# Sparse attention with a mixture of experts: preparation copies on GpSimd, and the first batch's causal mask as a matmul

## The chip, the cores and the metric

The kernel runs on one core of one Trainium2 chip. The metric is the device time of one execution in microseconds (us), and the median of several runs is compared. The engines are named as in the profile: PE is TensorE (PEld its weight loads), DVE is VectorE, ACT is ScalarE, POOL is GpSimd, and SP issues most DMAs. Each engine works through its own queue in order; semaphores tie the queues together.

## The reference

There are 4 batches of 8 heads with 768 positions of 64 features. Keys stand in 24 chunks of 32. A query takes only the 6 chunks with the highest upper bound of a score, and of these only keys that are not later than itself:

```python
ub = np.sum(np.maximum(q[:, :, :, None, :] * k_min[:, :, None, :, :], q[:, :, :, None, :] * k_max[:, :, None, :, :]), axis=-1)
top_chunks = np.argsort(np.where(causal, ub, -1e9), axis=-1)[..., -top_k:]
mask = sel & (pos[:, None] >= pos[None, :])
attn = softmax(np.where(mask, scale * q @ k.T, -1e9))
x = (attn @ v).transpose(0, 2, 1, 3).reshape(B * S, H * D)
y_dense = np.maximum(x @ w1_dense, 0.0) @ w2_dense
y_moe[e's tokens] = gate_w * (np.maximum(x @ w1[e], 0.0) @ w2[e])    # e: the best of 8 experts by x @ w_gate
return y_dense + y_moe
```

## The kernel before, in words

**Pairs and units.** Two heads are worked on together as a pair, so there are 16 pairs (`NP`), four per batch (`HP`). The scores of a pair are cut into 11 units of up to 512 columns. Units 0, 5 and 6 hold the diagonal blocks of 128 x 128, where the causal mask cuts through; each of them has four such blocks. For a unit PE computes the scores (line 551), ACT the exponential (555), POOL zeroes later keys in a diagonal unit with a select (557), and PE multiplies with the values (570). The main loop runs over all units; it starts the scores two units ahead and finishes a unit, with the value product, one unit late.

**Chunk selection without a mask of its own.** The score matmul has 128 rows of contraction: 64 features and, in the other 64 rows, 24 rows of chunk membership. `kT[i][g]` holds the keys of head g in one half and the membership table `exf` in the other; `rT[i][g]` holds the negated queries in one half and, in the other, a flag for each chunk that was not selected. Thus a key of an unselected chunk gets a large positive score, and the exponential with scale -0.125 makes it zero. There are three buffers of each (`NB`), used by pair p modulo 3. The membership rows are written once at the start (`expand`, 144 and 145).

**Preparation.** Pair p+2 is prepared while pair p runs. POOL casts k, q and v to f16 (469, 471, 476). `prep_k` transposes the keys on PE (482), ACT copies them from PSUM into `kp` (484), and DVE reduces every chunk to its maximum and minimum, `ks` (495), and multiplies them with a mask of halves into `kb` (498). `prep_q` transposes the queries (510); ACT writes their positive part `qp` (513), and DVE writes the negated queries into `rT` (514 for all 128 partitions, 515 for the second head's half). `prep_kt` copies both halves of `kp` into `kT` on DVE (502, 503). `prep_ub` computes the bounds on PE (525), finds the sixth largest with DVE (531) and writes the flags (533). `prep_s`, a pair later, transposes the flags (539) and copies them into `rT` (541, 542).

**Other work in the loop.** A finished pair is normalized on DVE (579, 581). The dense layer and the gate of a batch are mixed as small pieces into the units of the next batch. POOL also scatters the tokens into a table by expert (370), issues the expert weights' loads (206), and builds the routing constants once (171 to 186). After the attention the experts' blocks run; their results are scattered by POOL (733).

**Order.** A scheduler of the language orders each engine's instructions from the program order, with its own estimates of duration. `tc.issue_after(latest["pool"].ins)` ties the casts and the table scatters behind the POOL instruction that the program made last, which before is the select of line 557.

## Time and profile before

| | |
|---|---|
| time, median of 3 runs | 255.95 us (254.11 to 255.99) |
| the profiled execution's own time | 257.31 us |
| its span, first to last instruction | 255.5 us |
| mean granted clock of TensorE | 0.993 |
| busy: PE / DVE / ACT / POOL | 213.7 / 179.3 / 176.1 / 159.6 us |
| DMA | 50.12 MB moved |

Busy time is what an engine's instructions took; PE's is modelled, because matmuls are pipelined. A group of instructions is one source line with its operation and shapes; behind it stand the busy time, the mean duration of one in ns, the idle time of the engine just ahead of them, and what ended that idle time. The chain of waits is followed back from the last instruction to whatever released each step. In a timeline row the first two numbers are the start and the duration in us.

### The profile page before, as it was taken

Reading aid. Unit: us, or ns where it says so; the run is one execution under the profiler, and the core shown is the slowest. Engines: PE = TensorE matmul, PEld = TensorE weight load, DVE = VectorE, ACT = ScalarE, POOL = GpSimd, SP = SyncE. Lnnn points to the kernel's source line nnn. Section 1 sums busy time; section 2 is a strip of 40 time slices with the busy share of each in tenths; the row PEclk is TensorE's granted clock in tenths of the full one; section 3 lists DMA queues with packets and bytes.
Section 4 is the critical chain, followed back from the end, with each engine's and each line's share of the span. In section 5 each row is a group of like instructions: output and inputs, shape, how many; then the busy total and the mean of one; then the engine's idle time right before and its main releaser. Section 6 shows DMA issues by size and latency. Waiting matters only on the chain.

```text
span 255.5 us, 7236 instructions
## 1 busy us (share of the span) xinstructions
PE 213.7 (84%) x2547; PEld 141.8 (55%) x2547; DVE 179.3 (70%) x558; ACT 176.1 (69%) x332; POOL 159.6 (62%) x198
## 2 busy tenths in 40 slices
PE   0378969888989899999988988889769999999970
PEld 0256746656657576766567755555335554555530
DVE  6869989999979689998898895167223345555540
ACT  2799979878779898878889778815356555455440
POOL 4746998566276987168986145514744463887881
PEclk9999999999999999999999999999999999999997
DMA  6999999999999799989999924447879999787885
GB/s 172 262 267 228 217 227 239 220 232 202 239 174 292 132 276 226 250 179 242 298 230 258 190 72 128 144 114 218 234 154 208 220 209 200 124 140 97 117 112 105
DMA packets 75124, 50.12 MB, mean 196 GB/s; under 512 B 29648, under 2 KB 68176, under 8 KB 75088
## 3 DMA queue, kind: packets, MB, share of 16 engines
q1 hardware_dynamic: 59856, 30.33, 46.9%
q0 software_dynamic: 15232, 19.32, 45.6%
q8 instruction: 21, 0.34, 0.6%
q14 instruction: 15, 0.12, 0.1%
HBM read 41.93 MB, written 18.23 MB: 235 GB/s over the span
## 4 chain that ended last, share of the span: by engine, by line
PE 29%; DVE 22%; POOL 18%; issue 10%; DMA 7%; ACT 6%; SPq 3%; another core or an unknown queue 1%; POOLq 0%; DVEq 0%; ACTq 0%
DVE ks L495 7%; POOL out_dram L733 7%; PE hp L696 6%; PE yp L725 6%; PE hp L385 4%; POOL ex L557 3%; PE yp L394 3%; POOL table L370 2%; SPq L92 2%; DMA vf<-in_v_dram 2%; ACT ex L555 2%; ACT kp L484 2%; DVE kT L503 2%; DMA kf<-in_k_dram 2%; PE sp L551 2%
## 5 line engine op out<-in xcount | busy, mean ns | idle before, releaser
L555 ACT ACTIVATE ex<-sp 128x512 f16<-128x512 f32 (+1 forms) x176 | 90.9, 608 | 8.9 <-PE sp L551 4.6
L551 PE MATMUL sp<-rT,kT 128*128 128x128 f16 (+3 forms) x384 | 64.4, 260 | 4.0 <-ACT ex L555 2.7
L733 POOL DMA_INDIRECT out_dram<-yo,xg x28 | 43.3, 1545 | 23.5 <-DVE yo L732 9.8
L557 POOL TENSOR_SCALAR_AFFINE_SELECT ex<-ex 128x512 f16<-128x512 f16 x48 | 32.6, 694 | 36.9 <-ACT ex L555 30.8
L570 PE MATMUL op<-v,ex 128*128 128x65 f16 x672 | 48.4, 194 | 3.3 <-POOL ex L557 1.8
L570 PEld LDWEIGHTS <-ex 128*128 128x128 f16 x672 | 36.9, 98 | 19.0 <-POOL ex L557 6.4
L370 POOL DMA_INDIRECT table<-xbig,slot x24 | 23.9, 997 | 20.2 <-issue 15.1
L732 DVE TENSOR_SCALAR yo<-yp,xg 128x512 f32<-128x512 f32 x27 | 20.3, 751 | 22.2 <-PE yp L725 13.3
L551 PEld LDWEIGHTS <-kT 128*128 128x128 f16 x384 | 29.0, 98 | 7.7 <-issue 4.2
L725 PE MATMUL yp<-we,ehT 128*128 x112 | 28.7, 379 | 3.9 <-ACT ys L397 2.5
L707 ACT COPY ehT<-tp 128x512 f16<-128x512 f16 x28 | 16.4, 585 | 21.5 <-PE tp L705 16.7
L696 PE MATMUL hp<-we,exT 128*128 x112 | 29.1, 379 | 2.0 <-DMA xg<-table 1.2
L495 DVE TENSOR_REDUCE ks<-kp 128x24 f16<-128x768 f16 x30 | 27.3, 943 | 4.2 <-ACT kp L484 3.9
L385 PE MATMUL hp<-xT,wd 128*128 128x384 f16 x128 | 26.2, 325 | 0.8 <-DVE xT L258 0.8
L699 ACT ACTIVATE eh<-hp 128x512 f16<-128x512 f32 x28 | 16.7, 597 | 11.4 <-PE hp L696 10.1
L394 PE MATMUL yp<-wd,hT 128*128 128x512 f16 x96 | 23.9, 379 | 0.3 <-issue 0.3
L690 DVE COPY exT<-tp 128x512 f16<-128x512 f16 x28 | 11.8, 423 | 17.4 <-PE tp L688 9.9
L387 ACT ACTIVATE hT<-hp 128x384 f16<-128x384 f32 x32 | 16.1, 505 | 9.0 <-PE hp L385 6.2
L397 ACT COPY ys<-yp 128x512 f32<-128x512 f32 x24 | 14.3, 598 | 9.5 <-PE yp L394 4.3
L484 ACT COPY kp<-pk 128x768 f16<-128x768 f16 x16 | 12.9, 806 | 8.8 <-PE pk L482 8.8
L581 DVE TENSOR_TENSOR xbig<-op,rs 128x384 f16<-128x384 f32 x32 | 17.5, 547 | 0.2
L725 PEld LDWEIGHTS <-ehT 128*128 128x128 f16 x112 | 10.1, 98 | 12.6 <-issue 2.8
(127 smaller groups left out, 383.1 us busy)
## 6 DMA issues: line engine op xcount, KB each, us to landing
we<-in_moe_w_dram POOLq DMA_DIRECT2D x16, 512.0 KB
kf<-in_k_dram SPq DMA_DIRECT2D x32, 192.0 KB
qf<-in_q_dram SPq DMA_DIRECT2D x32, 192.0 KB
vf<-in_v_dram SPq DMA_DIRECT2D x32, 192.0 KB
out_dram<-ys SPq DMA_DIRECT2D x48, 128.0 KB
xg<-table SPq DMA_DIRECT2D x28, 136.0 KB
table<-zt SPq DMA_DIRECT2D x9, 136.0 KB
wd<-in_moe_w_dense_dram POOLq DMA_DIRECT2D x2, 512.0 KB
```

The costliest lines, as they stand in the source:

```text
L370: sc = nc.gpsimd.indirect_dma_start(out=table, out_offset=bass.IndirectOffsetOnAxis(ap=keep["slot"][:, t : t + 1], axis=0), in_=xbig[b % 2 ...
L385: nc.tensor.matmul(hp, wd[:, ko, j * 128 : (j + 1) * 128], xT[:, ko, g * G * 128 : (g + 1) * G * 128], start=(ko == 0), stop=(ko == NK - 1))
L394: nc.tensor.matmul(yp, hold["h"][:, j, i * 128 : (i + 1) * 128], wd[:, NK + j], start=(j == 0), stop=(j == NK - 1))
L495: nc.vector.tensor_reduce(out=ks[:, i], in_=kp.rearrange("d (c w) -> d c w", w=32), op=op, axis=mybir.AxisListType.X)
L551: nc.tensor.matmul(sp[:, o : o + w], kT[p % NB][g][:, kt * 128 : (kt + 1) * 128], rT[p % NB][g][:, a * 128 : z * 128], start=(o == 0), sto ...
L555: nc.scalar.activation(ex[:, 0:o], sp[:, 0:o], AF.Exp, scale=-0.125)
L557: latest["pool"] = nc.gpsimd.affine_select(out=ex, in_=ex, compare_op=ALU.is_ge, fill=0.0, base=0, pattern=[[0, 4], [1, 2], [2, 64]], chan ...
L570: nc.tensor.matmul(s["op", g][:, t * (D + 1) : (t + 1) * (D + 1)], ex[:, o : o + 128], v16[p % NB][:, g, kt, :], start=first, stop=(last_o ...
L696: nc.tensor.matmul(hp, s["xT"][:, ko], wef[:, bass.ds(offs[i] + ko * 512, 512)], start=(ko == 0), stop=(ko == NK - 1))
L725: nc.tensor.matmul(yp, s["hT"][:, j], wef[:, bass.ds(offs[i] + (NK + j) * 512, 512)], start=(j == 0), stop=(j == NK - 1))
L732: nc.vector.tensor_scalar(o, yp, gate, None, ALU.mult)
L733: sc = nc.gpsimd.indirect_dma_start(out=out, out_offset=to, in_=o, in_offset=None, bounds_check=N - 1, oob_is_err=False, compute_op=ALU.by ...
```

## The change

It has four parts.

1. In the first batch (pairs 0 to 3) the causal mask of a diagonal unit is added to the scores by one more matmul, of the identity with a table `later` that holds 30000 where the key is later than the query. It is repeated four times by its access pattern, so it covers 512 columns. The select on POOL goes for these pairs. From pair 4 on the select stays.
2. The keys are no longer written to a tile of their own, `kp`, but into `kT[..][1]`, all 128 partitions. From there the first head's half is copied to `kT[..][0]`: by POOL for pairs 1 to 3, by DVE for pair 0 and from pair 4 on. The first head's keys in `kT[..][1]` are then partly covered by the 32 membership rows; that copy from `exf` is made anew for each pair, by ACT for pair 0 and by POOL for the others. The rows that are left over meet zeros in `rT`.
3. The negated queries are written once, for all 128 partitions, into `rT[..][1]`. For pair 0 DVE writes the first head's half from PSUM again, and ACT computes the positive part as before. From pair 1 on DVE computes the positive part `qp` from `rT[..][1]` in SBUF, and POOL copies the first head's half to `rT[..][0]`. The third term of the bounds reads `rT[..][1]`.
4. With that go three memsets and three copies of `expand`. `latest["pool"]` now can also be one of the new POOL copies.

```diff
+    later = acst.tile([128, 128], HF)
+    nc.vector.memset(later, 0.0)
+    nc.gpsimd.affine_select(out=later, in_=later, compare_op=ALU.is_ge, fill=30000.0, base=0,
+                            pattern=[[1, NJ], [NJ, 64]], channel_multiplier=-1)
...
-            s["kp"] = kp = ahead.tile([128, S], HF, name="kp")
+            kp = kT[p % NB][1]
...
         def prep_kt(p):
-            kp = st[p]["kp"]
-            nc.vector.tensor_copy(kT[p % NB][0][0:64], kp[0:64])
-            nc.vector.tensor_copy(kT[p % NB][1][64:128], kp[64:128])
+            k0, k1 = kT[p % NB]
+            if p:
+                (nc.gpsimd if p < HP else nc.vector).tensor_copy(k0[0:64], k1[0:64])
+                latest["pool"] = nc.gpsimd.tensor_copy(k1[0:32], exf[0:32])
+            else:
+                nc.vector.tensor_copy(k0[0:64], k1[0:64])
+                nc.scalar.copy(k1[0:32], exf[0:32])
...
-            nc.scalar.activation(qp, pq, AF.Relu)
-            nc.vector.tensor_single_scalar(r0, pq, -1.0, ALU.mult)
-            nc.vector.tensor_single_scalar(r1[64:128], pq[64:128], -1.0, ALU.mult)
+            if p:
+                nc.vector.tensor_single_scalar(r1, pq, -1.0, ALU.mult)
+                nc.vector.tensor_scalar(qp, r1, -1.0, 0.0, ALU.mult, ALU.max)
+                latest["pool"] = nc.gpsimd.tensor_copy(r0[0:64], r1[0:64])
+            else:
+                nc.scalar.activation(qp, pq, AF.Relu)
+                nc.vector.tensor_single_scalar(r1, pq, -1.0, ALU.mult)
+                nc.vector.tensor_single_scalar(r0[0:64], pq[0:64], -1.0, ALU.mult)
...
+            diag = pc[0][1] == pc[0][2]
+            added = diag and p < HP
+            if added:
+                nc.tensor.matmul(sp.rearrange("p (n k) -> p n k", k=128), ident, later.unsqueeze(1).to_broadcast([128, 4, 128]),
+                                 start=True, stop=False, skip_group_check=True)
...
-            if pc[0][1] == pc[0][2]:
+            if diag and not added:
                 latest["pool"] = nc.gpsimd.affine_select(out=ex, in_=ex, compare_op=ALU.is_ge, fill=0.0, base=0,
```

More of the change, by code (lines that the diff above doesn't have):

```diff
@@ L133 @@
         nc.vector.memset(kT[i][0][64:128], 0.0)
-        nc.vector.memset(kT[i][1][0:64], 0.0)
         nc.vector.memset(v16[i][:, :, :, D : D + 1], 1.0)
@@ L551, in scores @@
                 nc.tensor.matmul(sp[:, o : o + w], kT[p % NB][g][:, kt * 128 : (kt + 1) * 128],
-                                 rT[p % NB][g][:, a * 128 : z * 128], start=(o == 0), stop=True, skip_group_check=True)
+                                 rT[p % NB][g][:, a * 128 : z * 128], start=(o == 0 and not added), stop=True,
+                                 skip_group_check=True)
                 o += w
```

5 lines of the change are left out of this document (2 added, 3 removed).

## The prediction

> **What bounds the kernel now.** I read the totals first, then the busy time by stretch, the waits, and the chain of waits.
>
> ```profile
> PE 213.7 (84%) x2547; PEld 141.8 (55%) x2547; DVE 179.3 (70%) x558; ACT 176.1 (69%) x332; POOL 159.6 (62%) x198
> ```
>
> The totals mix stages with different limits. The busy time by stretch separates them; columns are PE, PEld, DVE, ACT and POOL.
>
> ```profile
> core 0: us, PE busy (x) PEld busy (x) DVE busy (x) ACT busy (x) POOL busy (x), PEclk, DMA share, GB/s
> 16.00:46.00 30.00, 24.19 (x376) 17.03 (x374) 27.81 (x90) 26.78 (x52) 23.72 (x46) 1.00 1.15 228
> 46.00:72.00 26.00, 23.31 (x362) 17.33 (x360) 24.69 (x77) 19.94 (x40) 12.91 (x19) 1.00 1.03 217
> 72.00:102.00 30.00, 26.95 (x390) 19.77 (x388) 25.28 (x86) 26.54 (x53) 24.20 (x31) 1.00 1.00 226
> 102.00:131.00 29.00, 27.29 (x388) 19.28 (x385) 25.87 (x86) 24.68 (x50) 20.05 (x27) 1.00 1.09 238
> 131.00:160.00 29.00, 25.88 (x371) 18.83 (x368) 24.34 (x96) 23.71 (x49) 14.90 (x22) 1.00 0.82 170
> ```
>
> In the first batch (16 to 46) DVE is busy 27.81 of 30 us and ACT 26.78; PE has 5.81 idle. From 46 to 160, where the dense layer of the batch before is mixed in, PE is busy 103.43 of 114 us, DVE 100.18, ACT 94.87 and POOL 72.06. There PE leads and leaves 10.57 us of idle time: no relief of another engine can be worth more there. After 160 the change touches nothing.
>
> The chain of waits shows the first batch's loop. It comes round once per pair; every piece left out below is DVE too, except 0.52 us of transposes and some gaps.
>
> ```profile
> 38.49 0.56 DVE rT L541
> ...
> 42.43 0.56 DVE rT L515
> ...
> 43.01 0.35 DVE kT L502
> ...
> 43.37 0.76 DVE kT L503
> ...
> 46.26 0.56 DVE rT L541
> ```
>
> One round is 46.26 - 38.49 = 7.77 us, and three of its pieces, 1.67 us, belong to lines that the change edits. For the later pairs the waits of 50 to 165 us say what interrupts PE:
>
> ```profile
> PEld L539 <- DVE fl L533: 3.4, 4, 1.4
> ...
> PEld L570 <- POOL ex L557: 2.5, 7, 0.5
> ...
> PEld L510 <- DVE rT L542: 2.4, 2, 1.2
> ```
>
> Late DVE results cost PE's weight loads 5.8 us there, late masks 2.5 us.
>
> **The change part by part.** The durations are these groups, shapes kept apart:
>
> ```profile
> L557 POOL TENSOR_SCALAR_AFFINE_SELECT ex<-ex 128x512 f16<-128x512 f16 x48 | 32.6, 694 | 36.9 <-ACT ex L555 30.8 <-DMA kf<-in_k_dram 5.4 <-issue 0.4
> ...
> L513 ACT ACTIVATE qp<-pq 128x768 f16<-128x768 f16 x16 | 13.3, 829 | 0.5 <-PE pq L510 0.5
> L469 POOL CAST k<-kf 128x768 f16<-128x768 f32 x16 | 13.2, 825 | 3.1 <-DMA kf<-in_k_dram 3.1
> ...
> L515 DVE TENSOR_SCALAR rT<-pq 64x768 f16<-64x768 f16 x16 | 9.0, 561 | 0.5
> ...
> L503 DVE COPY kT<-kp 64x768 f16<-64x768 f16 x16 | 8.0, 500 | 0.3
> ...
> L502 DVE COPY kT<-kp 64x768 f16<-64x768 f16 x16 | 7.0, 437 | 0.1
> ```
>
> *ACT*, per pair from 1 on, loses the relu, 0.83 us. *DVE* loses the half negation (0.56) and, for pairs 1 to 3, both key copies (0.44 and 0.50), from pair 4 one of them (0.50). It gains the relu from SBUF, 128x768 f16. The trace has no such operation. It costs at least 0.35 us (the key copy that waits for nothing, 43.01) and at most 0.76 (the key copy 0.36 us later). I take 0.50, the mean of such a copy. So DVE gains 0.56 + 0.44 + 0.50 - 0.50 = 1.00 us in a preparation of pairs 2 and 3, and 0.56 us from pair 4 on; at 0.76 it is 0.74 and 0.30, at 0.35 it is 1.15 and 0.71.
>
> *POOL* gains, per pair from 1 on, the query copy and the member copy, each 768 elements long; pairs 1 to 3 also get the key copy. Nothing like an f16 copy on POOL is in the trace. The nearest row is the cast of 768 elements, 0.825 us, which I take; 0.35 (if POOL were as fast as DVE) and 1.24 (the cast plus the 0.41 that separates 0.76 from 0.35, if each is held up once) are the ends. That is 1.65 us more per later pair, 0.70 to 2.48. It loses the 12 masks of pairs 0 to 3, 12 x 0.694 = 8.3 us, against 3 x 2.48 = 7.4 us of copies for pairs 1 to 3.
>
> *PE* gains 12 matmuls of 512 columns and their weight loads. Back to back, eight such matmuls take
>
> ```profile
> 200.51 1.73 PE yp L394 x8
> ```
>
> so 0.216 us each, 12 x 0.216 = 2.6 us, all in the first batch. In a stage that PE does not bound they could cost nothing; 2.6 is the other end.
>
> *Prologue.* Three memsets and two copies by ACT go, a small memset and one select come. All lie beside the wait for the first loads; I cost them at nothing. If that wait were gone, it would be a few tenths, as a gain.
>
> **First batch.** Four preparations lie in it: pairs 2 and 3 in the time of pairs 0 and 1, pairs 4 and 5 in that of 2 and 3. On the DVE loop they give 2 x 1.00 + 2 x 0.56 = 3.1 us. Besides, POOL's block of routing constants no longer holds up a mask. Before, PE waited for it:
>
> ```profile
> 37.88 0.24 PE L570 MATMUL op<-v,ex 128*128 128x65 f16 x2 [1.20 <-POOL ex L557]
> ```
>
> Together 4.3 us. But PE has 5.81 us of room and takes 2.6 more, so it lets only 3.2 go. What is late next is PE, with ACT 4 x 0.83 shorter. Value taken: **-3.2**; ends: -4.3 (if PE's busy time is not its full rate) and -0.5 (if 2.6 lies on the path and DVE gains only 2 x 0.74 + 2 x 0.30 = 2.1, with the 1.2 kept by another wait).
>
> **Later pairs.** Ten preparations remain (pairs 6 to 15, in the time of pairs 4 to 13). DVE gets 5.6 and ACT 8.3 us shorter, but PE can only give back its waits for DVE, 5.8 us. I take a third, 2.0, since PE comes back to a queue of dense work anyway; ends 0 and 5.8.
>
> Against it stands POOL's queue. The masks of pairs 4 to 15 stay on it, and the built order mostly puts the query copy behind the last two masks of a pair, and the member copy ahead of the casts of k and q. The query copy waits for DVE's negation, the member copy for DVE's reductions and key copy. Queued behind them are casts, table scatters, weight loads and the next mask, for which the value matmuls on PE wait. This matters while the table is scattered, over two pairs in each of two batches. The second of these stretches begins and ends so:
>
> ```profile
> 111.86 1.03 POOL L370 DMA_INDIRECT table<-xbig,slot  x1 [1.43 <-issue]
> ...
> 129.49 0.66 POOL L557 TENSOR_SCALAR_AFFINE_SELECT ex<-ex 128x512 f16<-128x512 f16 x1 [0.72 <-ACT ex L555]
> ```
>
> Between these, POOL waits for ACT for only 0.72 us; two pairs bring 2 x 1.65 = 3.3, so its queue runs 2.6 us late. In the first stretch it waited longer:
>
> ```profile
> 80.30 0.87 POOL L557 TENSOR_SCALAR_AFFINE_SELECT ex<-ex 128x512 f16<-128x512 f16 x1 [1.72 <-ACT ex L555]
> ...
> 90.25 0.84 POOL L557 TENSOR_SCALAR_AFFINE_SELECT ex<-ex 128x512 f16<-128x512 f16 x1 [0.91 <-ACT ex L555]
> ```
>
> 1.72 + 0.91 = 2.63, so it is 0.7 late. Of these 3.3 us I let 2.3 reach PE, because a mask is used about one unit after it is made; ends 0 and 3.3 at this copy price, 6.6 if the query and member copies stop the queue for DVE as well. Outside these stretches POOL's own idle time covers the copies; without that cover they would be 1.65 a pair.
>
> One price of such company is visible already: DVE's copy at 43.37 lay beside two masks on POOL,
>
> ```profile
> 43.25 1.40 POOL L557 TENSOR_SCALAR_AFFINE_SELECT ex<-ex 128x512 f16<-128x512 f16 x2 [0.21 <-ACT ex L555]
> ```
>
> and took 0.76 instead of 0.35 us. [...]
>
> **Sum.** -3.2 - 2.0 + 2.3 = -2.9 us. The profiled execution took 257.31 us for its span of 255.5, 1.4 above the median of the three runs, 255.95; it would become 254.4, its span 252.6. From the median: 255.95 - 2.9 = **253.1 us**.
>
> **Rivals.**
> 1. *Slower: POOL's queue becomes the bound while the table is scattered.* For it: 0.72 us of slack against 3.3. Against it: 2.63 in the other stretch, and POOL is busy 72.06 of 114 us. If each copy also stops for DVE (1.24 us), two pairs bring 5.0 and the two stretches lose 4.2 and 2.3, 6.5 together; PE, waiting for masks, then gets nothing from DVE's relief. -3.2 + 6.5 = +3.3, 259.3 us. It decides from the point where two pairs' copies exceed the slack by more than the first batch's gain, at about 1.2 us a copy.
> 2. *The first batch gains little and the rest cancels.* The mask matmuls take PE's room: -0.5 instead of -3.2, with +0.3 later: 255.7.
> 3. [...] The relu, the key copy and the product kb, all on DVE, each wait for a POOL instruction, 0.41 us more: 1.23 a pair against 0.56 gained, so later pairs keep no relief, and the first batch half of its own: -1.6 + 2.3 = +0.7, 256.7. For it: 0.76 at 43.37, and the query copy on POOL starts exactly when DVE's relu is next. Against it: in some preparations the built order puts the two reductions between negation and relu, time enough for the copy to end.
> 4. *Larger gain.* PE gets all its waits for DVE back and masks slip by less: -3.2 - 5.0 + 1.0 = -7.2, 248.8. For it: ACT, too, becomes 8.3 us shorter. Against it: PE is busy 27.29 of 29 us in one stretch.
>
> **How the numbers follow.** Chances: forecast 0.40 (of this 0.30 beyond 1%), rival 1 0.23, rivals 2 and 3 together 0.25, rival 4 0.12. One per cent, 2.6 us, is about what a measurement of this kernel can tell from no change. So faster 0.30 + 0.12 = 0.42, same 0.10 + 0.25 = 0.35, slower 0.23. The range leaves out the outer half of rival 4 (below 249.5) and about half of rival 1 (above 258.6), under 0.2 together; the forecast's own is 250.5 to 255.
>
> **What would show it.** In the profile after: ACT's relu once, the SBUF relu on DVE near 0.5 us (0.35: free of POOL; 0.76: behind it); POOL copies near 0.83; a round of the first batch near 7 us; no wait of PE for POOL before 50 us; in the scatter stretches PE waiting for POOL's masks by some 2 us more. The prediction is wrong if PE's idle time between 16 and 46 does not shrink, if POOL's copies take over 1.2 us, or if the later pairs as a whole move by more than 3 us either way.

## The result, and the profile after

The changed kernel takes 269.89 us (median of 4 runs, 269.15 to 272.96) against 255.97 of the kernel before on the same chip: ratio 1.058, interval 1.049 to 1.068. The forecast of 253.1 and its range, 249.5 to 258.6, missed it. The profiled execution took 270.29 us, its span is 268.6.

The totals, the busy time in the stretches of the prediction, and the waits of 50 to 165 us, all of the kernel after:

```profile
PE 223.5 (83%) x2559; PEld 149.6 (56%) x2559; DVE 175.9 (65%) x537; ACT 166.5 (62%) x315; POOL 178.1 (66%) x220
```

```profile
core 0: us, PE busy (x) PEld busy (x) DVE busy (x) ACT busy (x) POOL busy (x), PEclk, DMA share, GB/s
16.00:46.00 30.00, 23.54 (x306) 17.73 (x305) 24.24 (x62) 18.25 (x36) 18.30 (x37) 0.84 0.98 193
...
102.00:131.00 29.00, 25.69 (x377) 19.28 (x375) 23.75 (x74) 21.50 (x43) 21.43 (x29) 0.96 0.97 216
131.00:160.00 29.00, 25.12 (x343) 18.26 (x341) 21.27 (x72) 20.16 (x40) 24.28 (x32) 0.93 1.15 232
```

```profile
PEld L589 <- POOL ex L576: 14.8, 15, 2.9
POOL rT L524 <- DVE rT L522: 11.9, 4, 4.9
...
PE op L589 <- POOL ex L576: 10.6, 12, 2.5
...
PEld L552 <- DVE fl L546: 1.2, 1, 1.2
```

Three things are new. In the first batch all engines became idler at once, and PE finished 306 matmuls in those 30 us instead of 376. The granted clock (the share of full speed at which PE may run), 1.00 in every one of these stretches before, is 0.84 there and 0.93 at the end. And in the later pairs PE's weight loads wait 14.8 us for POOL's masks; that was 2.5. Their waits for late DVE results went the other way, from the 5.8 us of the prediction to 1.2.

Where the time went is seen from the start of ACT's key copy of each pair (us from the span's start):

| | pair 4 | pair 6 | pair 9 | pair 15 | span |
|---|---|---|---|---|---|
| before | 38.8 | 56.1 | 85.3 | 145.4 | 255.5 |
| after | 46.3 | 61.1 | 94.2 | 159.9 | 268.6 |

The first batch lost 7.4 us (2.4 of them came back up to pair 6), the later pairs 9.5 more; after pair 15 1.4 came back.

**The first batch.** The rows of PE that waited longest there:

```profile
29.37 0.24 PE L538 MATMUL ub<-kb,qp 128*128 128x48 f16 x2 [3.41 <-DVE qp L523]
...
40.55 0.24 PE L538 MATMUL ub<-kb,qp 128*128 128x48 f16 x2 [2.79 <-DVE kb L501]
```

What DVE and POOL did ahead of the first of them (start, duration in us):

```profile
23.14 1.81 DVE L498 TENSOR_REDUCE ks<-kT 128x24 f16<-128x768 f16 x2
24.86 0.55 DVE L522 TENSOR_SCALAR rT<-pq 128x768 f16<-128x768 f16 x1
25.33 3.71 DVE L501 TENSOR_TENSOR kb<-ks,hmask 128x96 f16<-128x96 f16 x1
28.97 0.35 DVE L523 TENSOR_SCALAR qp<-rT 128x768 f16<-128x768 f16 x1
```

```profile
25.08 0.82 POOL L508 COPY kT<-exf 32x768 f16<-32x768 f16 x1 [1.09 <-DVE ks L498]
25.85 0.82 POOL L524 COPY rT<-rT 64x768 f16<-64x768 f16 x1
26.62 0.82 POOL L472 CAST k<-kf 128x768 f16<-128x768 f32 x1
27.39 0.82 POOL L474 CAST q<-qf 128x768 f16<-128x768 f32 x1
28.16 0.82 POOL L479 CAST v<-vf 128x768 f16<-128x768 f32 x1
```

DVE's product `kb`, 0.20 us where nothing is beside it, lasted 3.71 us and ended as POOL's row of five instructions ended (28.16 + 0.82 = 28.98). DVE's own reduction had released that row: the member copy waits for `ks`. A pair later `kb` lasted 3.13 us, again up to the end of a row that a reduction had released. In the kernel before no row of POOL is released by a reduction of DVE, and the longest `kb` is 0.74.

**The clock.** The granted clock is either 1.00 or 0.50 here, and its changes lie 3.41 us or a multiple of it apart. The changed kernel in windows of 3.4 us that follow these changes; the columns are the length, PE's busy time with its matmuls, the granted clock, the DMA share and GB/s:

```profile
26.00:29.40 3.40, 0.03 (x1) 1.00 0.19 53
29.40:32.80 3.40, 3.40 (x43) 0.50 1.26 248
...
36.30:39.70 3.40, 1.41 (x21) 1.00 1.09 179
39.70:43.10 3.40, 2.56 (x33) 0.50 0.91 244
43.10:46.50 3.40, 3.40 (x39) 0.50 1.10 206
125.00:128.40 3.40, 1.57 (x14) 1.00 0.91 213
128.40:131.80 3.40, 3.24 (x42) 0.50 1.07 157
142.10:145.50 3.40, 1.57 (x26) 1.00 1.21 208
145.50:148.90 3.40, 3.40 (x34) 0.50 1.07 300
```

Each of these windows in which PE did little is followed by one or two at half clock. That is no sharp rule: the window from 84.04 us, with PE busy for 1.71 us, is followed by full clock, and so is one with 1.53 us in the kernel before (from 187.14). Work at half clock takes about twice as long (a burst of 1.02 us takes 1.86, see below). So an estimate of what the half clock cost is half of PE's busy time in it: (3.40 + 2.56 + 3.40) / 2 = 4.7 us in the first batch, (3.24 + 3.40) / 2 = 3.3 in the later pairs. With the two waits, 3.41 + 2.79 = 6.2, that makes 10.9 us for the first batch. This is too much: a run below that takes the long `kb` away has pair 4 8.7 us earlier (37.6 instead of 46.3).

**The groups** that the sum had priced:

```profile
L501 DVE TENSOR_TENSOR kb<-ks,hmask 128x96 f16<-128x96 f16 x16 | 13.6, 848 | 0.0
L524 POOL COPY rT<-rT 64x768 f16<-64x768 f16 x15 | 13.1, 871 | 19.7 <-DVE rT L522 19.7
L508 POOL COPY kT<-exf 32x768 f16<-32x768 f16 x15 | 12.3, 822 | 3.9 <-DVE rs L598 1.6 <-DVE ks L498 1.3 <-DVE kT L507 0.8
...
L523 DVE TENSOR_SCALAR qp<-rT 128x768 f16<-128x768 f16 x15 | 7.5, 503 | 0.0
```

The relu (503 ns) and the POOL copies (871 and 822) cost what was taken, 0.50 and 0.825. The group that grew is `kb`, which the change does not touch: 848 ns, before 357. Half of its 13.6 us are the two long ones (3.71 + 3.13); from 50 to 166 us its mean is 499 ns.

### The profile page after: what moved, and what is told of

Its sections match the earlier page's. It is cut to its first block, busy times and chain, and to the rows that moved or that the text cites. A ratio compares the mean times of both kernels' runs of the same rounds, so it can differ in the third digit from the quotient of the medians.

```text
span 268.6 us, 7253 instructions
## 1 busy us (share of the span) xinstructions
PE 223.5 (83%) x2559; PEld 149.6 (56%) x2559; DVE 175.9 (65%) x537; ACT 166.5 (62%) x315; POOL 178.1 (66%) x220
## 4 chain that ended last, share of the span: by engine, by line
POOL 25%; PE 22%; DMA 17%; DVE 15%; issue 12%; ACT 5%; SPq 2%; POOLq 0%; DVEq 0%; ACTq 0%
DMA out_dram<-yo,xg 10%; POOL ex L576 5%; DVE ks L498 4%; PE hp L388 4%; POOL table L373 3%; POOL out_dram L752 3%; DVE kb L501 3%; PE hp L715 3%; DMA out_dram<-ys 3%; POOL k L472 3%; ACT ex L574 3%; PE sp L569 3%; POOL q L474 3%; DMA xg<-table 3%; POOL we L209 2%
## 5 line engine op out<-in xcount | busy, mean ns | idle before, releaser
L569 PE MATMUL sp<-rT,kT 128*128 128x128 f16 (+3 forms) x384 | 66.7, 272 | 1.1 <-ACT ex L574 0.5
L589 PE MATMUL op<-v,ex 128*128 128x65 f16 x672 | 51.0, 200 | 11.4 <-POOL ex L576 10.6
L589 PEld LDWEIGHTS <-ex 128*128 128x128 f16 x672 | 39.4, 102 | 29.1 <-POOL ex L576 14.8
L576 POOL TENSOR_SCALAR_AFFINE_SELECT ex<-ex 128x512 f16<-128x512 f16 x36 | 24.3, 685 | 13.3 <-ACT ex L574 13.1
L715 PE MATMUL hp<-we,exT 128*128 x112 | 30.1, 389 | 2.3 <-DMA xg<-table 1.4
L498 DVE TENSOR_REDUCE ks<-kT 128x24 f16<-128x768 f16 x30 | 27.3, 944 | 1.0 <-ACT kT L487 0.9
L524 POOL COPY rT<-rT 64x768 f16<-64x768 f16 x15 | 13.1, 871 | 19.7 <-DVE rT L522 19.7
L397 PE MATMUL yp<-wd,hT 128*128 128x512 f16 x96 | 24.8, 378 | 0.1
L487 ACT COPY kT<-pk 128x768 f16<-128x768 f16 x16 | 12.9, 804 | 11.7 <-PE pk L485 11.6
L538 PE MATMUL ub<-kb,qp 128*128 128x48 f16 x192 | 10.6, 192 | 9.0 <-DVE kb L501 5.6
```

What stands on the lines that cost most here:

```text
L397: nc.tensor.matmul(yp, hold["h"][:, j, i * 128 : (i + 1) * 128], wd[:, NK + j], start=(j == 0), stop=(j == NK - 1))
L498: nc.vector.tensor_reduce(out=ks[:, i], in_=kp.rearrange("d (c w) -> d c w", w=32), op=op, axis=mybir.AxisListType.X)
L569: nc.tensor.matmul(sp[:, o : o + w], kT[p % NB][g][:, kt * 128 : (kt + 1) * 128], rT[p % NB][g][:, a * 128 : z * 128], start=(o == 0 and n ...
L576: latest["pool"] = nc.gpsimd.affine_select(out=ex, in_=ex, compare_op=ALU.is_ge, fill=0.0, base=0, pattern=[[0, 4], [1, 2], [2, 64]], chan ...
L589: nc.tensor.matmul(s["op", g][:, t * (D + 1) : (t + 1) * (D + 1)], ex[:, o : o + 128], v16[p % NB][:, g, kt, :], start=first, stop=(last_o ...
L715: nc.tensor.matmul(hp, s["xT"][:, ko], wef[:, bass.ds(offs[i] + ko * 512, 512)], start=(ko == 0), stop=(ko == NK - 1))
```

## The experiments

Ratios are to the kernel before on the same chip.

### Each half alone

*First batch changed only.* Pairs 0 to 3 as in the changed kernel, the rest as before:

```diff
-            if p:
+            if p >= HP:
+                nc.scalar.activation(qp, pq, AF.Relu)
+                nc.vector.tensor_single_scalar(r0, pq, -1.0, ALU.mult)
+                nc.vector.tensor_single_scalar(r1[64:128], pq[64:128], -1.0, ALU.mult)
+            elif p:
```

> The first batch as changed (mask by matmul, preparations of pairs 1 to 3 with the GpSimd copies), pairs 4 to 15 prepared as before. Theory: in the changed kernel the product kb on DVE waits for a whole back-to-back run of POOL instructions (3.71 and 3.13 us instead of 0.2 to 0.7), PE idles behind it for 3.4 and 2.8 us, and its granted clock then falls to half. So kb should be long here as well, and the kernel about 5 to 7 us slower than before, 261 to 263. Rival, mask matmuls: the loss comes from their 2.6 us on PE alone, 257 to 259, with kb short and the clock full. Rival, later pairs: the whole loss comes from pairs 4 on, so this kernel is at 253 to 256.

Measured: 265.59 us, before 258.38; its four executions (260.41 to 267.3, so 2.0 to 8.9 us above) lie too far apart for an interval. In the one that was profiled, the 267.3, pair 4 starts at 46.0 us, with the same two waits and the same half clocks.

*Later pairs changed only* (the same condition turned round, and no mask matmul).

> The first batch as before (masks by POOL, copies by DVE, relu by ACT), the preparations of pairs 4 to 15 as changed. Theory: POOL's queue carries 1.65 us more per pair, the masks come late while the table is scattered, PE waits for POOL's masks some 8 us more than before, and the kernel is 7 to 9 us slower, 263 to 265. Rival, first batch: the later pairs cancel to within 2 us, 254 to 258. If the two parts are independent, the two differences add up to 13.9.

Measured: 265.23 us, ratio 1.025 (1.018 to 1.032). Pair 4 starts at 38.9, pair 15 at 152.0, 6.6 later than before.

So the later half alone costs 2.5%, 6 to 7 us, where the forecast had 0.3. The first half, forecast as a gain, is a loss in all four executions (260.41 at least, where the kernel before took 260.18 at most), but this run does not tell its size; the run that frees VectorE, below, does from the other side.

### What holds `kb` up

*`kb` made by ACT*, so that DVE has no product there:

```diff
-            nc.vector.tensor_tensor(kb, ks.unsqueeze(2).to_broadcast([128, 2, 2, NC]), hmask, ALU.mult)
+            for i in range(2):
+                for g in range(2):
+                    nc.scalar.activation(kb[:, i, g], ks[:, i], AF.Copy, scale=hsign[:, i, g])
```

> The changed kernel with the product kb taken from DVE to ACT, as four small scaled copies per pair, so that no DVE instruction with two SBUF inputs stands in the preparation. Theory of the run: the two waits of PE for kb in the first batch go, and with them the half clock there; 262 to 265 us, the first batch shorter by 5 to 7 us. Rival (kb was long because of something that comes from elsewhere, or the mask matmuls cost the time): the first batch keeps its length, 268 to 271.

Measured: 277.01 us, ratio 1.072 (1.065 to 1.079), outside both ranges. The delay went to the relu, now DVE's next instruction that works in SBUF:

```profile
26.56 3.76 DVE L528 TENSOR_SCALAR qp<-rT 128x768 f16<-128x768 f16 x1
...
38.53 4.78 DVE L528 TENSOR_SCALAR qp<-rT 128x768 f16<-128x768 f16 x1
```

So it is not a matter of the product with its two operands: the relu, with one, is held up as long.

*The row put behind `kb` and `qp`.* In the first batch the member copy and the first cast behind it wait for both:

```diff
                 latest["pool"] = nc.gpsimd.tensor_copy(k1[0:32], exf[0:32])
+                behind(p, latest["pool"])
```

> Edit: the changed kernel, but in the first batch (pairs 1 to 3) GpSimd's member copy and the first cast behind it (with all that stands behind them on GpSimd) wait until VectorE's kb and qp of the same pair are done; nothing else differs. Starvation theory (a VectorE instruction with SBUF operands asked for while GpSimd has several instructions ready waits until GpSimd's whole row of instructions has run out; the row begins because VectorE's own reduce releases the member copy): kb and qp last under 1 us in the first batch (3.71 and 3.13 us in the changed kernel, 3.76 and 4.78 with kb taken off VectorE), TensorE's waits for them (3.4 and 2.8 us) go, no half clock between 16 and 46 us, pair 4 starts near 40 to 42 us instead of 46.25, and the time falls by 5 to 7 us against the changed kernel, to 263 to 265. Rival (the long times are only the profile's way of showing a wait for something else, such as the cast's DMA or a semaphore): the long instructions stay, or move to another instruction again, time 268 to 272. Second rival (the casts now come too late): kb and qp are short, but TensorE waits for the casts k and q instead, over 2 us in sum, time 266 to 270.

Measured: 262.6 us, ratio 1.030 (1.018 to 1.041). No `kb` or `qp` of the first batch is over 0.87 us, and the first batch is now faster than before:

```profile
16.00:46.00 30.00, 28.45 (x429) 21.27 (x428) 26.63 (x89) 25.55 (x51) 23.60 (x42) 1.00 1.02 196
```

Pair 4 starts at 37.6 us, pair 6 at 52.9, 3.2 before the 56.1 of the kernel before. So the row on POOL is what lost the first batch its time. Against the changed kernel pair 4 starts 8.7 us earlier, and the ratio falls from 1.058 to 1.030, about 7 us; what is left is near the later half's 1.025. The lead itself does not last: pair 7 starts at 66.9 us, 0.8 behind the kernel before.

*The same, with the later pairs as before.*

> Edit: only the first batch is changed (as in the first-batch run), and in it GpSimd's member copy and first cast wait for VectorE's kb and qp (as in the run that put GpSimd's row behind them); the later pairs are those of the kernel before. There pair 6 began at 52.9 us against 56.1 before, 3.2 us ahead. Theory (the forecast saving of the first batch is real once VectorE is not kept out): pair 4 at 37 to 38 us, pair 6 at 52.5 to 54 us, all later pairs 2 to 3.5 us earlier than before, time ratio 0.985 to 0.992, 252 to 254 us. Rival (the lead is lost again in the later pairs, where VectorE is as busy as it was and the DMAs of keys, queries and values have not become earlier): pair 8 level with before, ratio 0.997 to 1.005.

Measured: 259.95 us, ratio 1.004 (1.001 to 1.007), as the rival had it. Pair 4 starts at 36.7 us, 2.2 ahead, and pair 6 at 56.3, 0.2 behind. The lead ends at a load: POOL's cast of v waits for it, the mask stands behind the cast, PE waits for the mask, and a half clock follows (54.8 to 58.3 us). One row of POOL, one of PE:

```profile
51.02 0.83 POOL L481 CAST v<-vf 128x768 f16<-128x768 f32 x1 [3.05 <-DMA vf<-in_v_dram]
```

```profile
53.28 0.24 PE L607 MATMUL op<-v,ex 128*128 128x65 f16 x2 [2.79 <-POOL ex L594]
```

*The contention alone*, in three measurements with nothing of the kernel around it. First, DVE instructions beside one to eight POOL copies, casts, selects or memsets:

> A kernel that leaves out the whole computation and only measures: POOL gets n copies back to back (n = 0, 1, 2, 3, 4, 6, 8; 64x768 f16), and into their run DVE starts one instruction, the product of two SBUF tiles (128x96) or the SBUF copy (64x768); then with four POOL casts, selects or memsets; then a relu from SBUF, a reduction and a copy from PSUM against four POOL copies. Theory of the run: the product's time grows by about 0.77 us with each copy, to 3 us for 4 and 6 us for 8; the reduction and the PSUM copy keep their own times (0.94 and 0.4). Rival (one instruction): the product waits for the POOL instruction that is running and for no other, 0.2 to 1.0 us whatever n is. For the SBUF copy the theory leaves both open: 0.35 to 0.83 in some preparations and 1.18, two instructions, in others.

Measured: a product beside any number of copies lasts 0.20 us, a copy beside four selects 0.78, none over 1 us. Then the point was varied at which DVE asks:

> Measures alone (the kernel's computation is left out). First half: GpSimd runs either four copies (64x768) or the kernel's own row (32-partition copy, 64-partition copy, three 128x768 casts from float32), and VectorE asks for kb (product with a broadcast operand), qp (multiply and max, 128x768) or a copy (64x768), after a PSUM copy of 8 to 768 columns, so at eight delays of about 0.1 to 1.1 us after GpSimd's first instruction began. Starvation theory: the ones that ask well before GpSimd's first instruction ends last until the row has run out (2.3 us or more for four copies, 3 us or more for the kernel's row), the ones that ask as it ends (as the 0.20 us products of the run before did) are short. Rival (one instruction at most is waited for): none over 1 us. Second half: TensorE in bursts of 47 to 55 matmuls of 512 columns, with gaps made of 1 to 8 VectorE copies from PSUM (about 0.8 to 5.5 us), each twice, then 4 matmuls per gap of one copy, of two and of three. Clock theory A (a window of 3.4 us must be wholly idle): half clock only after gaps of 3.4 us or more. Theory B (a window of low activity is enough): half clock already after gaps of 1.7 to 3 us, or in the dense pattern of short gaps.

Measured: all 48 under 1.0 us (0.99 at most); those that waited came in as the POOL instruction that was running ended (the product of 14.77 us, beside a copy from 14.72, took 0.83). Then rows that wait for nothing after their first copy:

> Measures alone (the kernel's computation is left out). GpSimd runs a row of five 64x768 copies to tiles of their own, of which only the first waits (for VectorE); VectorE asks for kb, qp or a 64x768 copy at three delays inside the first copy. Then rows in which small copies that wait for GpSimd's own earlier copy stand between. In the measurement before this one every copy after the first also waited for GpSimd's own semaphore, and VectorE came in at the next boundary each time; in the kernel the casts of the long rows wait for DMAs and TensorE only. Theory O (GpSimd keeps VectorE out from one instruction to the next unless it has to wait in between): kb, qp and copy last until the row has run out, 3.0 to 3.8 us, in the first nine trials, and under 1.2 us in the rows with waits. Rival (what the next instruction waits for does not matter): all under 1 us; what keeps VectorE out in the kernel is then something else.

Measured: 0.57 to 0.92 us in all twelve. So "DVE waits for the whole row" is no general rule, and for rows of plain copies it makes no difference whether they wait for POOL's own copies. The exact sequence of the kernel was next:

> Measures alone (the kernel's computation is left out). ScalarE's key copy, VectorE's two reduces, r1 from PSUM, kb and qp, and GpSimd's member copy (released by the reduces), query copy and three rearranging casts, with the kernel's shapes, orders and operands, in seven variants (twice as in the kernel's pair 2; as in pair 3; kb and qp swapped in each; without the member copy; without the casts); first quiet, then again beside 48 loads of 256 KB and a stream of matmuls. Theory Q (the sequence itself keeps VectorE out): kb or qp lasts 2.5 us or more in most of the quiet variants that have the casts. Theory T (the traffic beside it does): under 1.2 us when quiet, 2.5 us or more beside the loads. Rival: under 1.2 us in both; then it is something that these measurements do not hold, and stays open.

Measured, alike to 0.02 us whether the loads and matmuls run beside it or only the stores of the output: 3.72 us in the order of pair 2, 3.76 with `qp` first, at most 0.91 and 1.09 where the reductions come after r1 (the negated queries of both heads), 1.40 without the casts, at most 0.36 without the member copy. So the sequence itself does it, without the traffic of the kernel. Its parts were varied last:

> Measures alone (the kernel's computation is left out). The sequence reduces, r1 from PSUM, kb beside GpSimd's member copy, query copy and three casts, in ten variants, each twice: as it is; the query copy from a fixed tile instead of r1; without the query copy; r1 from float32 PSUM at half the speed; that with the fixed tile; with a PSUM copy of 8, 128 or 256 columns between r1 and kb; with one cast and the query copy; with one cast and without it. Theory W (a GpSimd instruction in the row that waits for VectorE's r1 is what keeps kb out): kb 3.0 to 3.8 us as it is, under 1 us with the fixed tile and without the query copy. Theory F (the fast r1 from 16-bit PSUM right ahead of kb does): under 1 us with the float32 r1 and with a copy between, 3 us or more with the fixed tile. Theory D (what counts is how deep in GpSimd's first instruction kb asks): kb's time changes with the copy between, and with nothing else.

DVE's product in the first three variants (as it is; query copy from a fixed tile; no query copy), and then in the one with one cast:

```profile
10.93 3.73 DVE L93 TENSOR_TENSOR kb<-ks,hm 128x96 f16<-128x96 f16 x1
17.05 0.71 DVE L93 TENSOR_TENSOR kb<-ks,hm 128x96 f16<-128x96 f16 x1
23.13 0.68 DVE L93 TENSOR_TENSOR kb<-ks,hm 128x96 f16<-128x96 f16 x1
...
58.91 2.17 DVE L93 TENSOR_TENSOR kb<-ks,hm 128x96 f16<-128x96 f16 x1
```

With an r1 read more slowly, from float32 (0.68 us for 512 columns; the other takes 0.55 for 768), it is 3.59, and 0.58 if the query copy also reads the fixed tile. This fits theory W: with a query copy that waits for DVE's r1, which is not done when the row begins, `kb` lasts until the row is out, whatever else is varied; without it, up to the end of one POOL instruction. In the kernel:

```diff
-                latest["pool"] = nc.gpsimd.tensor_copy(r0[0:64], r1[0:64])
+                if p < HP:
+                    nc.vector.tensor_copy(r0[0:64], r1[0:64])
+                else:
+                    latest["pool"] = nc.gpsimd.tensor_copy(r0[0:64], r1[0:64])
```

> Edit: the changed kernel, but the query copy of pairs 1 to 3 (r1's lower half to r0) is made by VectorE (0.34 us each, behind kb and qp) instead of GpSimd; nothing waits for anything new. Theory W (the query copy's wait for r1, inside GpSimd's row, keeps VectorE out): pair 2's kb and qp last under 1 us (3.71 in the changed kernel), pair 4 starts 3 to 6 us earlier than 46.25, ratio to before 1.03 to 1.045 instead of 1.058. If other waits in a row do the same (pair 3's row of member copy and casts has no query copy, and its kb took 3.13 us): pair 3's kb or qp still lasts over 2 us, and a half clock follows it. Rival (any long row keeps VectorE out in the kernel): both stay, pair 4 at 45 to 48 us, ratio 1.05 to 1.065.

Measured: 269.76 us, ratio 1.064 (1.056 to 1.073), near the last rival: both long `kb` stay, and pair 4 starts at 44.4 us. `kb` still lasts to the end of the row, which is one instruction shorter:

```profile
25.14 2.94 DVE L501 TENSOR_TENSOR kb<-ks,hmask 128x96 f16<-128x96 f16 x1
...
35.37 3.13 DVE L501 TENSOR_TENSOR kb<-ks,hmask 128x96 f16<-128x96 f16 x1
```

Here the instruction behind the member copy is a cast that waits for its load and for PE. So the query copy is one way to it and not the only one. That the row on POOL holds DVE up is shown; which rows do so stays open: a second instruction that waits for another engine or a load fits the long cases, but in the kernel before DVE came in between two masks that wait for ACT (the 0.76 us at 43.37, quoted in the prediction).

### What the clock costs

The second half of the phase run drives PE alone. Bursts of 4 matmuls, 1.02 us each, with gaps of 0.78 us; then the same with gaps of 1.51 us:

```profile
479.23 1.02 PE L108 MATMUL pg<-mv,id__79 128*128 128x512 f16 x4 [0.78 <-DVE slow L112]
...
496.51 1.02 PE L108 MATMUL pg<-mv,id__79 128*128 128x512 f16 x4 [1.51 <-DVE slow L112]
499.04 1.86 PE L108 MATMUL pg<-mv,id__79 128*128 128x512 f16 x4 [1.51 <-DVE slow L112]
```

Busy for 57% of the time (1.02 of 1.80) PE keeps the full clock, busy for 40% (1.02 of 2.53) it loses it and gets it back only in the long burst that follows (15.51 us for 64 matmuls; behind the gaps of 0.78 they took 13.97): theory B. With single gaps it can go either way: both bursts behind a gap of 2.96 us were slower (13.72 us instead of 12.03, and 11.99 instead of 10.30), of those behind a gap of 3.68 only one (13.59 instead of 12.03; the other took the full-clock 10.30). An estimate says why. The clock's changes in this run lie multiples of 3.41 us apart, one of them at 378.8 (the burst from 378.68 us lost 1.69 us, about half of 3.41). Counted from there, the gap of 3.68 us that cost nothing (390.67 to 394.35) is cut near its middle by a boundary of the clock's windows, about 392.5, and PE was busy for some 1.6 us in the one window and 1.5 in the other; the gap that cost 1.6 us fills a window from end to end.

*The waits filled.* In the changed kernel PE runs matmuls that add +1 and -1 to the same result while it waits, so that they cancel:

```diff
+            for i in range({2: 22, 3: 18}.get(p, 0)):
+                nc.tensor.matmul(ub.rearrange("p t g c -> p (t g c)"), ident,
+                                 (minus if i % 2 else plus).rearrange("p t g c -> p (t g c)"),
+                                 start=False, stop=False, skip_group_check=True)
```

> Edit: the changed kernel, but where TensorE waited 3.41 and 2.79 us for qp and kb in the first batch, it first runs 22 and 18 matmuls of 288 columns that add +1 and -1 in turn to the same PSUM tile (nothing else differs). They stand behind the bias matmul, so in the wait itself. Clock theory (half clock follows a stretch in which TensorE did little; the half clock is worth as much as the wait): no half clock from 29 to 47 us, pair 4 starts 3 to 4.5 us earlier than 46.25, time 265 to 267 against 269.9. Rival (the half clock costs little, because VectorE sets the pace there anyway): pair 4 within 1 us of 46.25, time 269 to 272.

Measured: 272.6 us, ratio 1.058 (1.047 to 1.070), as without the filling. In its profile the second wait is followed by full clock and the first, where the filling ran out, is not:

```profile
25.10:28.50 3.40, 1.39 (x12) 1.00 0.02 4
28.50:31.90 3.40, 2.94 (x38) 0.50 0.77 220
...
35.30:38.70 3.40, 3.20 (x33) 1.00 1.03 156
38.70:42.10 3.40, 2.78 (x51) 1.00 1.22 231
```

Pair 4 starts at 43.8 us, 2.5 earlier; (2.56 + 3.40) / 2 = 3.0 was the estimate for the half clock that is gone. Some of the 2.5 may come from `kb`, which lasted 2.38 us here instead of 3.13. So the clock can be kept by filling the wait, and its price is at most about what the windows say. The whole time did not follow: the lead at pair 15 is 4.6 us, but in this execution the experts' stage, from the first to the last start of the matmuls with the experts' first weights, took 78.8 us against 75.5 after and 77.3 before. What sets that stage was not studied.

### The later pairs

*The same copies without their waits*: the query copy reads a fixed tile, the member copy writes rows that are there already.

```diff
-                latest["pool"] = nc.gpsimd.tensor_copy(r0[0:64], r1[0:64])
+                latest["pool"] = nc.gpsimd.tensor_copy(r0[0:64], fixed[0:64])
...
-                latest["pool"] = nc.gpsimd.tensor_copy(k1[0:32], exf[0:32])
+                latest["pool"] = nc.gpsimd.tensor_copy(k0[64:96], exf[0:32])
```

> Edit: the kernel with only the later pairs changed (265.23 us, TensorE waiting 8.7 us for GpSimd's masks, GpSimd 12.4 us for r1 ahead of the query copy), but GpSimd's query copy of a later pair reads a fixed tile instead of r1 and its member copy writes the same values to rows of the other key tile that hold them already: GpSimd runs the same number of instructions of the same kinds and sizes and waits for VectorE in none of them. (It leaves the query's lower half and the member rows out of the later pairs' sums.) Queue theory (masks come late because a copy that waits for VectorE stands ahead of them in GpSimd's order): TensorE's wait for the masks falls to 2 to 4 us, time 256 to 260. Load theory (GpSimd has too much to do in the scatter stretches, whoever releases the copies): the waits for masks stay at 6 to 9 us, time 263 to 266.

Measured: 259.89 us, ratio 1.021 (1.008 to 1.034), on another chip than the 265.23: the kernel before takes 255.38 us on this one, 258.38 on that one. So the ratio is the better measure, and it is in the load theory's range (263 / 258.38 = 1.018 and more), as the waits are: PE still waits 9.9 us for masks, 8.7 with the copies' waits. Pair 15 starts at 148.8 us, half way between 152.0 and 145.4, but the times of the two kernels (1.021 and 1.025) cannot be told apart.

*The member copy on ACT* (`nc.scalar.copy(k1[0:32], exf[0:32])`).

> Edit: the kernel with only the later pairs changed (ratio 1.025 to before, TensorE waiting 8.7 us for masks), but the member copy of a later pair is made by ScalarE instead of GpSimd: GpSimd loses 12 copies of 0.82 us; ScalarE, busy 20 to 21 of 27 to 30 us there, gains 12 of some 0.5 us. The copies with fixed operands had brought back about half of the loss. Load theory: half or more of the loss comes back, ratio 1.005 to 1.015, waits for masks 4 to 6 us. Queue theory (the query copy that waits for r1 is what holds the masks): little comes back, ratio 1.018 to 1.028, waits for masks 7 to 9 us.

Measured: 272.54 us, ratio 1.052 (1.046 to 1.058), worse than either theory. The copy must wait for DVE to have read those rows, and the exponentials stand behind it. Nor was it one of "some 0.5 us": in the kernel before ACT's copies of 32x768 from `exf` took 0.83. The waits of ACT, 50 to 166 us:

```profile
ACT kT L507 <- DVE kT L506: 8.6, 6, 3.1
```

*The query copy on DVE.*

> Edit: the kernel with only the later pairs changed, but the query copy of a later pair (r1's lower half to r0) is made by VectorE instead of GpSimd: GpSimd loses 12 copies of 0.82 us and with them all its waits for r1 (12.4 us), VectorE gains 12 of 0.34 us. Queue theory: nearly all of the loss comes back, ratio 0.995 to 1.008, waits for masks 2 to 4 us. Load theory: about as much as with the member copy taken off, ratio 1.005 to 1.015, waits 4 to 6 us.

Measured: 264.51 us, ratio 1.025 (1.019 to 1.030): nothing comes back, though POOL no longer waits for r1 and waits 27.8 us for ACT instead (23.5 before). Both ranges are missed. But the load theory is not refuted: the 27.8 us are a sum over 116 us, and the longest of these waits (5.88 us) ends at 113.00, just ahead of the second scatter stretch. From 114.7 to 140.9 POOL waits for no other engine, and the masks are still late (6.8 us).

The same is seen where the query copy is still on POOL. One round of its queue in the second scatter stretch, from one pair of masks to that of the next pair, in the kernel before and in the changed kernel:

```profile
115.01 1.30 POOL L557 TENSOR_SCALAR_AFFINE_SELECT ex<-ex 128x512 f16<-128x512 f16 x2
...
124.59 1.33 POOL L557 TENSOR_SCALAR_AFFINE_SELECT ex<-ex 128x512 f16<-128x512 f16 x2
```

```profile
127.17 1.33 POOL L576 TENSOR_SCALAR_AFFINE_SELECT ex<-ex 128x512 f16<-128x512 f16 x2
...
138.37 1.31 POOL L576 TENSOR_SCALAR_AFFINE_SELECT ex<-ex 128x512 f16<-128x512 f16 x2
```

Nothing between these rows waits for another engine. The round takes 9.58 us before, 11.20 in the changed kernel, and 10.45 with the query copy on DVE (121.25 to 131.70): the copies lengthen a queue that had no room. That this run gains nothing by its shorter round may be the clock: up to 166 us its profile has three half clocks of 3.41 us, the one with the query copy on POOL has one. This was not separated.

*The key half alone* and *the query half alone*, the rest as before:

> Edit: the first batch as before; of the later pairs only the key half of the change (ScalarE's copy goes straight into the second key tile, one VectorE copy, the member copy on GpSimd); the query half is that of the kernel before. If the member copy in GpSimd's queue (which waits for VectorE's copy and reduce of the pair) is what costs: ratio 1.015 to 1.025, TensorE's waits for masks 5 us or more after 50 us. If the query half is what costs: ratio 0.997 to 1.008, waits for masks under 3 us.

Measured: 263.1 us, ratio 1.017 (1.010 to 1.024), and PE waits 8.1 us for masks: the member copy in POOL's queue costs most of the 2.5% by itself. DVE's `kb` and key copy are as short as before (378 and 424 ns).

> Edit: the first batch as before; of the later pairs only the query half of the change (r1 whole from PSUM, the relu from r1 on VectorE, the query copy on GpSimd); the key half is that of the kernel before. If the query copy and the longer chain to the relu cost: ratio 1.012 to 1.025, waits for masks 5 us or more, GpSimd waiting 8 us or more for r1. If the key half is what costs: ratio 0.995 to 1.008. If the two halves cost only together (GpSimd's queue just full with both): both ratios under 1.01.

Measured: 270.64 us, ratio 1.047 (1.038 to 1.055), more than both halves together. Here PE waits for DVE, as its longest wait and DVE's groups from 50 to 166 us show:

```profile
PE ub L538 <- DVE kb L500: 8.1, 7, 2.1
```

```profile
L500 DVE TENSOR_TENSOR kb<-ks,hmask 128x96 f16<-128x96 f16 x11 | 10.0, 906 | 0.0
...
L523 DVE TENSOR_SCALAR qp<-rT 128x768 f16<-128x768 f16 x11 | 7.3, 662 | 0.0
```

In the same stretch `kb` took 341 ns before and the two key copies 444 and 529; here it is 906, 572 and 732, and the relu 662. That is 0.56 + 0.13 + 0.20 = 0.9 us more a pair than before, on the engine that the change was to relieve. With both halves in, as in the run of the later pairs, it is not so: there `kb` takes 514 ns and the one key copy 436. So the halves do not add up; why the key half shortens `kb` again was not studied. What makes the masks late when both are in is, by these traces, the length of POOL's queue while the table is scattered. How much of the loss each copy and each half clock makes was not separated.

### The mask matmul alone

The kernel before with part 1 of the change and nothing else.

> Edit: the kernel before, with the first batch's masks added by a matmul and nothing else of the change. TensorE gains 12 matmuls of 0.22 us, 2.6 us, in the first batch; GpSimd loses 12 masks of 0.65 us there. Theory that the copies on GpSimd did the harm: no instruction of VectorE over 1.2 us, clock full from 16 to 46 us, time 254.5 to 259 (TensorE has 5.8 us of idle time there). Theory that the mask matmul itself harms (longer chain into the exp, or the clock): half clock in the first batch, time 260 to 264.

Measured: 255.43 us, ratio 0.999 (0.993 to 1.004): the 12 matmuls on PE and the 12 selects that left POOL make no difference together. No version was found that beats the kernel before.

## Why the prediction was wrong

- **First batch, -3.2.** The step that failed is the price of a DVE instruction beside POOL: "at least 0.35 us ... and at most 0.76", and in rival 3 "each wait for a POOL instruction, 0.41 us more". The bound came from one row, where DVE waited for one mask; it was no bound. `kb`, which had no term in the sum because the change leaves it alone, lasted 3.71 and 3.13 us. That the member copy waits for DVE's reductions was noted for the later pairs alone; in the first batch this makes the row begin just as `kb` is next. With the row put behind DVE's instructions 8.7 us come back at pair 4. Nor is the 0.41 what was left of a mask: by the two masks' 1.40 us the first had some 0.58 left when the copy began (43.25 + 0.70 - 43.37).
- **The clock** had no term. It has a part in both halves: by the windows, as an estimate, up to 4.7 us behind PE's waits in the first batch and 3.3 in the later pairs.
- **The saving itself.** With DVE freed, pair 6 does start 3.2 us early once, but that it equals the forecast is luck: the lead is 1.2 us at pair 4 and gone at pair 7. PE's room, 5.81 - 2.6, was taken as what bounds it. With the later pairs as before, a load ends the lead, and nothing of it is left (ratio 1.004).
- **Mask matmuls, 2.6, or nothing** in a stage that PE does not bound: nothing, together with the selects that go (0.999).
- **POOL copies 0.825, relu 0.50**: 0.871 and 0.822, and 0.503. Right. **The prologue**, taken as nothing: pair 1 starts 0.4 us earlier, at 14.69 against 15.10.
- **Later pairs, -2.0 + 2.3.** Measured alone they cost 2.5%, 6 to 7 us. The term that failed is the +2.3 for late masks. PE's waits for POOL's masks grew from 0.6 to 10.6 us, and 8.5 of these lie in the scatter stretches and right behind them (2.50 us at 85.63, 1.82 at 127.93, 1.67 at 144.92). That is rival 1, in direction, place and mechanism: POOL's queue is the bound while the table is scattered. Its size was not: the prediction set the copies of two pairs against POOL's few waits for ACT, as a backlog that is paid once, but a round that had no room becomes 1.62 us longer each time, and half clocks follow. Rival 1's limit, "about 1.2 us a copy", was also wrong by its own numbers: eight copies less 0.72 and 2.63 us of slack exceed the 3.2 of the first batch from 0.82 us on, the price that was taken.
- **DVE's relief, -2.0** of 5.6: the pieces that the change touches, with `kb`, took 0.56 + 0.44 + 0.53 + 0.34 = 1.87 us a pair before and 0.56 (relu) + 0.54 + 0.50 = 1.60 after, from 50 to 166 us. So half of the 0.56 a pair was there. The waits of PE's weight loads for DVE fell by 4.6 us (5.8 to 1.2), more than the 2.0; how much of this is the relief, and how much is hidden behind the waits for masks, the trace does not tell. In the query half alone the relief turns round, by 0.9 us and more, as rival 3 has it; in the changed kernel it does not.
- **Of the signs named beforehand** two were met: PE's idle time between 16 and 46 us grew (5.81 to 6.46), and the later pairs moved by 9.5 us.

That a DVE instruction waits for one POOL instruction and no more ("each wait for a POOL instruction, 0.41 us more") was an assumption with one row behind it, the 0.76 us at 43.37. The rows of plain copies measured alone agree with it (at most 0.99 us); the kernel's row of five does not (3.71 us in the kernel, 3.72 measured alone), and there the measurement decides.

## What to carry to other kernels

Before a copy is moved to GpSimd, ask what releases it and what VectorE has next at that moment: a copy that VectorE itself releases, with a row of ready casts behind it, can keep VectorE out for the length of the row (3.71 us for a product that takes 0.20 alone). Price a wait of TensorE together with the clock that may follow it: in these runs half clock came, though not every time, when about half or more of a window of 3.41 us was left idle (1.83 of 3.40 us from 125.00 on in the changed kernel). Look for the receiving engine's idle time in the stretch where its queue is fullest, not on average: GpSimd was busy for 72.06 of 114 us, but a round of its queue in a scatter stretch had no wait in it. And the copy should be ready when its turn comes; the later pairs cost 2.5% with the member copy on GpSimd and 5.2% with it on ScalarE, whose exponentials then stood behind its wait.

## What the runs showed of the hardware that was not expected

- VectorE was kept out through four or five GpSimd instructions (2.94 to 3.76 us; 4.78 through memsets too), repeatable to 0.02 us in the sequence alone, and let in after one in sequences that differ only in what the second of them reads (3.73 against 0.71 us).
- TensorE's clock halved after windows of 3.41 us with some work in them. 1.57 of 3.40 us busy was too little, and so was 40% in short bursts; 57% in short bursts was enough. There is no sharp limit of busy time between: 1.53 us was enough once in the kernel before, while 1.57 was too little twice in the changed one. The clock's changes lie 3.41 us or a multiple of it apart (the half clocks in the changed kernel are 3.41 us or twice that), and a gap as long as a window is not needed: gaps of 1.51 us, repeated, were enough.
